# q before k in the attention by seven products: the order of the phases, the copies of q, and the queue of the bound's broadcast

## The chip, the cores and the metric

The kernel runs on one core of a Trainium2 chip. The metric is device time in microseconds of one execution. The times shown are those of three runs; the profile is one further execution, taken by the hardware profiler. The engines are named as in the profile: PE (TensorE) multiplies matrices, DVE (VectorE), ACT (ScalarE) and POOL (GpSimd) work on elements, SP (SyncE) only issues transfers. ACT, POOL and SP issue DMAs in the order of their own instruction streams: an instruction that waits holds up everything behind it on its engine.

## The reference

The input x has 2048 rows (tokens) of 1024. Four residual steps are applied to it: attention, token mixer, attention, token mixer, with the same weights both times.

```python
x = x + _A_ref(_layernorm(x, axis=-1), A_wqkv, A_wo)
x = x + _B_ref(_layernorm(x, axis=-1), B_w1, B_b1, B_w2, B_b2)
```

and the same two lines once more. `_A_ref` is attention with 32 heads of 32, in which a token sees itself and the seven tokens at distances 2, 4, ... 14 before it. Even and odd tokens therefore never meet, and the kernel treats them as two classes of 1024 tokens. `_B_ref` multiplies along the token axis: 2048 tokens to 3584 hidden units, gelu, and back.

## The kernel before

**Stages.** In the order of time: start-up with v of the first layer (0 to 64 us of the span), first attention (to 204), its output projection and layer norm (to 262), first `gemm1` (to 430), `gemm2f` (to about 620), the second layer's v and attention (to about 800), the last visits and the rest of the output projection (to 860), second `gemm1` (to 1032), `gemm2s` (to the end). Matrix products from the first `gemm1` on, and q, k and v of the second layer, are computed as Strassen-like schemes: seven products of half-size blocks in place of eight, with sums of blocks made beforehand on DVE and POOL, and partial results moved between PSUM banks by ACT.

**The second attention** is class `Attention` (L533). It works through NP = 8 periods. In period p two phases run, one for q and one for k, each for 256 columns (two groups of four heads) of one class of tokens. A phase is the seven products P1, P5, P6, P2, P7, P3 and P4, of four matmuls each (L652). ACT copies the bank of one product into the next bank before it is added to (`ab` and `pc`, L717), makes `Z` (L720), and writes out the corner blocks `c11` and `c21` (L724); DVE writes `y12` and `y22`, which add `Z` (L725). The four results of k go straight into their tile (`kT` or `kx`). The four results of q go into one tile `qs`, from which they are copied by DMA into the two buffers `qB` (L679): each result by four transfers, one a head, into that head's own place, since the rest of qB must stay zero. A DVE copy `hq` (L685) adds eight columns to the first buffer that lie over the border between its halves.

Between the products stand the visits of the pair before: in period p the steps S1 to S4 are the score products (L812) of the four visits of pair p - 1, `e` their exponentials on ACT (L820), `m` the multiplications by the band mask on DVE, four a visit (L836), V the products with v (L861 to L874), `l` and `x` the reciprocal of the sums on ACT, `n` the division on DVE (L887). V lags S by two visits. S1 and S2 read the first buffer qB (halves c11 and y12), S3 and S4 the second (c21 and y22). The four `t` steps of the first four periods make the block sums for the second class of tokens (L568).

**What sets the order.** The strings PE, ACT, DVE, SP and POOL (L535 to L539) give the order of the steps on each engine within a period, written out by hand; "-" means the step of the period before. `needs` (L589) tells which steps must be issued before a step, and `cycle` (L633) merges the strings accordingly. Each engine's instructions are chained in that order. Waits between engines are then set by the tile framework from what the instructions read and write. On POOL, `wk` and `wq` load the next weights and their sums (L571 to L576, two transfers of 512 KB each), which were stored to DRAM by `keep` (L527) ahead.

Before the change, k's phase comes first in a period: P1k, P4q of the period before, P5k, S1, V1, P6k, P2k, P7k, S2, V2, P3k, P1q, P4k, P5q, S3, V3, P6q, P2q, P3q, S4, V4, P7q. `last_visits` (L995) continues by hand after the last period: the remaining steps of period 7, then the output projection of the first eight tiles between the last visits. `out_proj` (L916) loads a residual tile `xr` three tiles ahead of its use.

**The bound's broadcast** belongs to the first `gemm1` (L1303). Its w1 blocks are scaled to fp16 by a power of two. For each block fb, DVE takes the maximum of both halves (`top`, L1322, two reductions); `share(fb)` (L1325) stores the 128 x 2 maxima to DRAM (`mxd`) and reads them back to all partitions (`bc`); one block later `power` reduces bc on DVE (L1233) and ACT scales the weights (L1332). Both transfers of `share` are issued by SP, whose queue also carries the loads of w1 (L1178), the stores of sums (L1348) and the loads for the second matrix's bound (L1286).

Of the kernel before, what the change touches and what calls it, by code (L numbers as in the profile page):

```python
# [9 lines left out]
ACT = mybir.ActivationFunctionType  # L10
# [7 lines left out]
P = 128  # L18
# [10 lines left out]
def kernel(  # L29
# [15 lines left out]
    nc = tc.nc  # L45
# [8 lines left out]
    NI = SC // P  # L54
    NG = D // P
# [442 lines left out]
    TURN = (2, 3, 0, 1)  # L498
# [33 lines left out]

    class Attention:  # L533
        NP = 4 * NG // 4
        PE = "P1k P4q- P5k S1 V1 P6k P2k P7k S2 V2 P3k P1q P4k P5q S3 V3 P6q P2q P3q S4 V4 P7q"  # L535
        ACT = "abk c21q- Zk e1a e1b l1 pck x1 e2a c11k l2 x2 abq e2b c21k e3a e3b l3 pcq x3 c11q Zq e4a l4 x4 e4b"
        DVE = ("n1 y22k m10 m11 y12k m12 n2 m13 m20 t1 m21 m22 m23 n3 m30 m31 y12q y22q hq m32 n4 m33 m40 t2 m41 m42 m43")
        SP = "dc21q- dc11q dy12q dy22q"
        POOL = "wk wq wx"  # L539

        def __init__(self):
# [26 lines left out]
            return tt(nc.vector, self.t_home(c, n)[:, ks], x[:, ks], y[:, ks], ALU.subtract)  # L568

        def load(self, phi):  # L570
            n = 2 * TURN[phi // 2 % (NG // 2)] + phi % 2  # L571
            ts = [wp.tile([P, KD, 256], FP16, name="Aq", tag="w"), wp.tile([P, 4, 4, P], FP16, name="Bq", tag="w")]
            self.w[phi] = [t[:] for t in ts]
            chain_("POOL", lambda: nc.gpsimd.dma_start(out=ts[0][:], in_=sdq[n][0]))
            chain_("POOL", lambda: nc.gpsimd.dma_start(out=ts[1][:].rearrange("p a k c -> p (a k c)"),
                                                       in_=sdq[n][1].rearrange("p k c -> p (k c)")))  # L576

        def take(self, phi, blocks):
            n = 2 * TURN[phi // 2] + phi % 2
            self.w[phi] = [blocks.R[n][:].bitcast(FP16), blocks.S[n][:]]  # L580

        def start(self, v, oT, wo):
# [5 lines left out]

        def needs(self, n, p):  # L589
            k, f = n[:-1], n[-1]  # L590
            o, d = ("q", p - 1) if f == "k" else ("k", p)
            if n[0] == "d":
                return [(n[1:], p)]
            if n[0] == "w":
                return {"x": [], "k": [("P4q", p - 1)], "q": [("P4k", p)]}[f]
            if n == "hq":
                return [("y12q", p)]
            if f in "kq":
                r = {"P1": [("c11" + o, d)], "ab": [("P1" + f, p), ("y12" + o, d)], "P5": [("Z" + o, d)],
                     "Z": [("P5" + f, p), ("y22" + o, d), ("y12" + o, d)], "P6": [("ab" + f, p)],  # L600
                     "pc": [("P6" + f, p), ("c21" + o, d)], "P2": [("ab" + f, p)], "P7": [("pc" + f, p)], "P3": [("pc" + f, p)],
                     "c11": [("P2" + f, p)], "y22": [("P7" + f, p), ("Z" + f, p)], "y12": [("P3" + f, p), ("Z" + f, p)],
                     "P4": [("y22" + f, p)], "c21": [("P4" + f, p)]}[k]
                if f == "q" and k in ("c11", "y12", "y22", "c21"):
                    r.append(("d" + n, p - 1))
                if k == "P1":
                    r.append(("wq", p - 2) if f == "k" else ("wk", p - 1))
                return r
            if n[0] == "t":
                return [("P5q", p)] if p == 3 else []  # L610
            c = n[1]
            o, d = {"1": ("4", p - 1), "2": ("1", p), "3": ("2", p), "4": ("3", p)}[c]
            if n[0] == "V":
                j = (int(c) - 3) % 4
                e = p - (c in "12")
                return [(f"m{j + 1}{r}", e) for r in range(4)] + [("l" + o, d), ("n" + o, d)]
            return {"S": [("e" + o + "a", d), ("e" + o + "b", d), ("dc11q", p - 1), ("dy12q", p - 1), ("hq", p - 1)]
                    + ([("dc21q", p - 1), ("dy22q", p - 1)] if c in "34" else []),
                    "e": [("S" + c, p)], "m": [("e" + c + "a", p), ("e" + c + "b", p), ("V" + c, p)],
                    "l": [("V" + c, p)], "x": [("l" + c, p)], "n": [("x" + c, p)]}[n[0]]  # L620
# [37 lines left out]
        def one(self, e, n, p):  # L658
            if e == "PE":
                in_order(self.do, n, p)  # L660
            elif n[0] == "d":
                self.do(n, p)
            else:
                chain_(e, self.do, n, p)
            self.done.add((n, p))
# [6 lines left out]
        def do(self, n, p):  # L672
# [24 lines left out]
            if f in "kq":  # L697
                ci_ = civ[:, 1:2]
                c = p // (NG // 2)
                bk = x.setdefault((f, p), {})  # L700
                if n[0] == "P":
                    A, B = self.w[2 * p + (f == "q")]
                    m = n[1]
                    if m in "15":
                        bk["pa" if m == "1" else "pd"] = bank("s")
                    lhs, rhs, out = {"1": (lambda: A[:, 0:4, 0:P], lambda: self.raw(c, 0, 0), "pa"),
                                     "2": (lambda: A[:, 4:8, 0:P], lambda: self.raw(c, 1, 0), "pa"),
                                     "5": (lambda: B[:, 0], lambda: self.t_home(c, 1), "pd"),
                                     "6": (lambda: B[:, 1], lambda: self.t_home(c, 2), "pb"),
                                     "7": (lambda: B[:, 2], lambda: self.t_home(c, 3), "pc"),  # L710
                                     "3": (lambda: B[:, 3], lambda: self.raw(c, 1, 1), "pb"),
                                     "4": (lambda: A[:, 4:8, P:2 * P], lambda: self.t_home(c, 4), "pc")}[m]
                    return self.product(bk[out][:], lhs(), rhs(), m in "15")
                if k in ("ab", "pc"):
                    o, i = ("pb", "pa") if k == "ab" else ("pc", "pb")
                    bk[o] = bank("m")
                    return nc.scalar.copy(out=bk[o][:], in_=bk[i][:])  # L717
                if k == "Z":
                    bk["z"] = x2("z", [P, 512], FP32)
                    return nc.scalar.activation(out=bk["z"][:], in_=bk["pd"][:], func=ACT.Identity, scale=ci_)  # L720
                a, b = int(k[1]) - 1, int(k[2]) - 1
                dst = self.place(f, p, a, b)
                if k[0] == "c":
                    return nc.scalar.activation(out=dst, in_=bk["pc" if a else "pa"][:], func=ACT.Identity, scale=ci_)  # L724
                return nc.vector.scalar_tensor_tensor(out=dst, in0=bk["pc" if a else "pb"][:], scalar=ci_, in1=bk["z"][:],  # L725
                                                      op0=ALU.mult, op1=ALU.add)
# [184 lines left out]
    def load_xr(res, e="SP"):  # L911
        t = gop.tile([P, D], BF16, name="xr", tag="go")
        xrs.append(t)
        chain_(e, lambda: (nc.sync if e == "SP" else nc.gpsimd).dma_start(out=t[:], in_=res(*todo.pop(0))))

    def out_proj(c, i, oT, wo, res, dst, h2, place=False):  # L916
        xr = xrs.pop(0)
        if todo:
            load_xr(res)
        if place:  # L920
            h2[c][i] = vhp.tile([P, D], BF16, name="h2", tag="vh")
        xn = h2[c][i] if place else x2("xn")
# [72 lines left out]
    def last_visits(at, v, oT, wo, res, dst, h2):  # L995
# [56 lines left out]
            chain_("DVE", divide, *divmod(z + n, 2), oT, accs[n], rds[n])  # L1052

        one = at.one
        one("DVE", "y22q", d)
        one("SP", "dy22q", d)
        one("DVE", "m32", d)
        one("DVE", "n4", d)
        o(0, 0)
        one("PE", "P4q", d)  # L1060
        one("ACT", "c21q", d)
        one("SP", "dc21q", d)
        a(0, 0)
        one("DVE", "m33", d)
        one("DVE", "hq", d)
        o(0, 1)
        a(0, 1)
        for r in range(4):
# [234 lines left out]
    def gemm1(h2, g, first):  # L1303
# [19 lines left out]
                                           apply_absolute_value=True)  # L1323

        def share(fb):  # L1325
            nc.sync.dma_start(out=mxd[fb], in_=bx[fb][:])
            bc_[fb] = pcp.tile([P, P * DIL], FP32, name="bc", tag="pc")
            nc.sync.dma_start(out=bc_[fb][:], in_=mxd[fb].rearrange("p c -> (p c)").partition_broadcast(P))

        def scale_w(fb, c):  # L1330
            w = w1s[fb][c]
# [660 lines left out]
    for li in range(2):  # L1992
# [77 lines left out]
        else:  # L2070
# [39 lines left out]
            at.late = {6: first_rows}  # L2110
            for k in range(2):
                at.take(2 + k, blocks[0])
                blocks[0].keep(6 + k, "POOL")
            oT = [None] * NG
            at.start(v, oT, wo)
            at.load(4)
            for p, e, m, j in ((p, f"t{j + 1}", m, j) for p, m in enumerate((3, 1, 2, 4)) for j in range(2)):
                at.extra[e, p] = lambda m=m, j=j: at.t_sum(1, m, j)
            for p in range(at.NP):
                if 1 <= p <= NG // 2:  # L2120
                    for k in range(2):
                        oT[2 * TURN[p - 1] + k] = gop.tile([P, S], BF16, name="oT", tag="go")
                if p == at.NP - 1:
                    at.DVE = at.DVE[:at.DVE.index(" y22q")]
                    at.SP = at.SP[:at.SP.index(" dy22q")]
                at.cycle(p)
            ahead_tiles = 8
            last_visits(at, v, oT, wo, res, xa[li], h2)
# [75 lines left out]
```

## Time and profile before

| | us |
|---|---|
| runs shown | 1204.96, 1208.30, 1208.88 |
| median | 1208.30 |
| profiled execution | 1207.63 |
| its span | 1205.9 |
| PE busy | 1174.4 |
| DVE busy | 804.9 |
| ACT busy | 741.6 |
| POOL busy | 157.7 |

The span is the time from the first to the last instruction in the profile; the 1.7 us around it belong to the execution. Of the stages, busy time of PE against length:

| stretch, us | length | PE busy |
|---|---|---|
| 262 to 430, first `gemm1` | 168.0 | 164.9 |
| 620 to 800, second attention | 180.0 | 166.0 |
| 800 to 860 | 60.0 | 57.4 |
| 860 to 1032, second `gemm1` | 172.0 | 171.3 |

A profile line of the timeline gives start, length, engine, line of the kernel, operation, output and inputs, and in brackets the idle time of that engine before it and what ended it. "PE s L812" is a matmul of line 812 that writes a bank named s. A releaser "DMA qB<-qs" is the landing of a transfer from qs to qB. "issue" means that the profile shows nothing that ended the wait.

### The profile page before, as it was taken

The numbers are of one execution on the slowest core, as the hardware profiler recorded it, in microseconds if no ns is written. First come the engines' busy times: TensorE is split into PE (matmuls) and PEld (weight loads), VectorE is DVE, ScalarE is ACT, GpSimd is POOL, SyncE is SP. The second block draws the span as 40 slices with busy tenths as digits, with TensorE's granted clock in tenths as the row PEclk, the third lists the DMA queues.
The fourth block names the chain that finished last, engine by engine and source line by source line (L and its number), as shares of the span: only waits on it lengthen the run. The fifth ranks groups of instructions, "written<-read, shape, count | busy, mean of one in ns | idle before, by whom it ended". The sixth has DMA issues, their size and how long they took to land.

```text
span 1205.9 us, 20563 instructions
## 1 busy us (share of the span) xinstructions
PE 1174.4 (97%) x7773; PEld 542.7 (45%) x7908; DVE 804.9 (67%) x1541; ACT 741.6 (61%) x1236; POOL 157.7 (13%) x159
## 2 busy tenths in 40 slices
PE   9999999999999999999999898999999999999998
PEld 4444444444444444444444344444444444444444
DVE  7558887887777546957678488787833432784663
ACT  4767876678878776665668477877543434432342
POOL 0000000281000031000040111201911212100000
PEclk9999999999999999999999899999999999999999
DMA  8922233696666778975465645535867755175521
GB/s 231 162 62 71 74 111 93 211 280 166 188 213 181 210 197 189 219 183 152 144 184 218 211 125 152 173 105 163 282 194 207 226 163 155 56 192 140 153 74 35
DMA packets 255859, 197.33 MB, mean 164 GB/s; under 512 B 50128, under 2 KB 226640, under 8 KB 252432
## 3 DMA queue, kind: packets, MB, share of 16 engines
q1 hardware_dynamic: 250912, 178.45, 53.6%
q0 software_dynamic: 4848, 17.57, 4.4%
q8 instruction: 62, 1.02, 0.4%
q14 instruction: 37, 0.30, 0.1%
HBM read 142.88 MB, written 38.82 MB: 151 GB/s over the span
## 4 chain that ended last, share of the span: by engine, by line
PE 88%; DMA 5%; ACT 2%; DVE 2%; issue 2%; SPq 1%; DVEq 0%; ACTq 0%
PE s L1356 11%; PE m L775 9%; PE m L927 8%; PE m L1356 7%; PE s L1565 7%; PE a L1356 6%; PE s L1715 5%; PE m L1565 4%; PE m L654 4%; PE a L1565 3%; PE s L654 3%; PE m L1715 3%; PE s L1195 2%; PE s L300 2%; PE s L450 2%; PE s L1808 2%
## 5 line engine op out<-in xcount | busy, mean ns | idle before, releaser
L836 DVE TENSOR_TENSOR Pm<-pc,band 32x640 bf16<-32x640 bf16 x256 | 125.2, 489 | 27.0 <-ACT pc L820 21.1
L1356 PEld LDWEIGHTS <-Sw 128*128 128x128 f16 x832 | 81.4, 98 | 100.9 <-issue 2.0
L775 PE MATMUL m<-hT,wqk 128*128 128x512 bf16 x481 | 111.8, 379 | 3.1 <-issue 2.2
L927 PE MATMUL m<-wo,oT 128*128 128x512 bf16 x497 | 111.3, 379 | 1.2 <-issue 0.5
L1356 PEld LDWEIGHTS <-w 128*128 128x128 f16 (+1 forms) x624 | 61.1, 98 | 73.6
L820 ACT ACTIVATE pc<-s,shift 128x320 bf16<-128x320 f32 x128 | 62.1, 527 | 28.6 <-PE s L812 28.1
L927 PEld LDWEIGHTS <-oT 128*128 128x128 bf16 x512 | 49.3, 98 | 60.8 <-issue 2.9
L775 PEld LDWEIGHTS <-wqk 128*128 128x128 bf16 x512 | 47.6, 98 | 59.0 <-issue 5.3
L1356 PE MATMUL s<-T,Sw 128*128 128x512 f16 x288 | 66.2, 379 | 1.9 <-ACT s L1365 1.9
L1209 POOL TENSOR_TENSOR Pm<-g 128x512 f16<-128x512 bf16 x24 | 28.6, 1208 | 285.8 <-ACT Pm L1290 165.8
L1209 DVE TENSOR_TENSOR py<-pz,m 128x512 f32<-128x512 f32 x14 | 9.6, 688 | 77.2 <-PE m L1356 63.1
L1209 POOL TENSOR_TENSOR T<-h 128x512 f16<-128x512 bf16 x16 | 18.4, 1152 | 288.3 <-ACT h L988 232.7
L887 DVE TENSOR_TENSOR oT<-a,rd 128x512 bf16<-128x512 f32 x64 | 44.2, 691 | 16.6 <-ACT rd L882 15.4
L1356 PE MATMUL m<-T,Sw 128*128 128x512 f16 x224 | 52.9, 379 | 0.4 <-ACT m L1365 0.4
L1356 PE MATMUL a<-h,w 128*128 128x512 bf16 x218 | 51.6, 379 | 0.4
L1332 ACT ACTIVATE w<-w,cs 128x2048 f16<-128x2048 bf16 x26 | 51.8, 1997 | 0.0
L1209 DVE TENSOR_TENSOR xs<-tq,xs 128x512 bf16<-128x512 f32 (+1 forms) x30 | 21.9, 732 | 44.3 <-ACT tq L1720 27.1
L1322 DVE TENSOR_REDUCE mx<-w 128x1 f32<-128x2048 bf16 x22 | 49.5, 2277 | 2.1 <-DMA w<-in_B_w_dram 2.0
L1565 PEld LDWEIGHTS <-u 128*128 128x128 f16 x336 | 32.9, 98 | 39.6
L1356 PE MATMUL s<-h,w 128*128 128x512 bf16 x186 | 44.1, 379 | 0.3
L1371 ACT ACTIVATE g<-pz,b_sb,ci 128x512 bf16<-128x512 f32 x26 | 21.1, 813 | 36.4 <-DVE pz L1209 36.4
L1209 DVE TENSOR_TENSOR py<-pz,s 128x512 f32<-128x512 f32 x12 | 8.3, 688 | 52.8 <-PE s L1356 43.7
(308 smaller groups left out, 2476.7 us busy)
## 6 DMA issues: line engine op xcount, KB each, us to landing
w<-in_B_w_dram SPq DMA_DIRECT2D x110, 512.0 KB, 6.0
sd<-Sw SPq DMA_DIRECT2D x13, 1024.0 KB, 8.1
Sw<-sd SPq DMA_DIRECT2D x13, 1024.0 KB, 4.9
xs<-xa SPq DMA_DIRECT2D x32, 256.0 KB, 3.3
Pm<-in_B_w_dram SPq DMA_DIRECT2D x26, 256.0 KB, 6.2
xa<-xn SPq DMA_DIRECT2D x24, 256.0 KB, 3.9
Aq<-sdq POOLq DMA_DIRECT2D x12, 512.0 KB, 3.8
Bq<-sdq POOLq DMA_DIRECT2D x12, 512.0 KB, 5.5
```

The source lines that it names most:

```text
L654: r = nc.tensor.matmul(out, lhsT=lhs[:, k, :], rhs=rhs[:, k, :], start=start and k == 0, stop=k == 3, skip_group_check=True)
L775: mm = nc.tensor.matmul(ps[:], lhsT=wts[part][:, kt, (g % 2) * P:(g % 2 + 1) * P], rhs=hT[:, kt, lo:lo + 512], start=(kt == 0), stop=(kt = ...
L820: return nc.scalar.activation(out=pc[:, 2 * n:2 * n + 2].rearrange("p t h k -> p (t h k)"), in_=ss[n][:, 0:2 * HG * GW], func=ACT.Exp, sca ...
L836: return nc.vector.tensor_tensor(out=Pm[rp, :, s0:s0 + HB, r * KG:r * KG + GW].rearrange("p h t k -> p t h k"), in0=pc[rp], in1=mk, op=ALU ...
L887: return nc.vector.tensor_tensor(out=oT[g][:, lo:lo + HB * P], in0=acc[0][:], in1=rd[:], op=ALU.mult)
L927: mm = nc.tensor.matmul(ps[:], lhsT=oT[g][:, cols(c, i)], rhs=wo[n][g // 4][:, g % 4, :], start=(g == 0), stop=(g == NG - 1))
L1209: return eng.tensor_tensor(out=out, in0=a, in1=b, op=op)
L1322: return nc.vector.tensor_reduce(out=bx[fb][:, c:c + 1], in_=w1s[fb][c][:], op=ALU.max, axis=AX.XY, apply_absolute_value=True)
L1332: return nc.scalar.activation(out=w[:].bitcast(FP16), in_=w[:], func=ACT.Identity, scale=cs[:, fb + 1:fb + 2])
L1356: r = nc.tensor.matmul(out, lhsT=lhs[:, k, :], rhs=rhs[k], start=start and k == 0, stop=stop and k == NI - 1, skip_group_check=True)
L1565: r = nc.tensor.matmul(out, lhsT=lhs[k], rhs=rhs[k][:, cols_], start=start and k == 0, stop=k == K - 1, skip_group_check=True)
L1715: r = nc.tensor.matmul(out, lhsT=lhs[k], rhs=rhs[k], start=start and k == 0, stop=k == K - 1, skip_group_check=True)
```

## The change

In `Attention`, q and k change places in every string and rule. q's phase runs first in a period, k's second; the weights are loaded and taken in that order (`load`, `take`). The copies of q are issued by SP in the order c21 and y22 of the period before, then c11 and y12 of this period, and `needs` places the first two behind S4 and the other two behind S2. `hq` moves ahead of m20 and behind S2. The block sums of the last kind (m = 4) take the places t2 and t3, the last at the end of DVE's string. `last_visits` issues the copies of c21 and y22 first and finishes k's y22 and c21 where q's were. One residual load in `out_proj` goes to POOL's queue. In `gemm1`, `share` issues its two transfers on POOL's queue for fb > 3, that is for ten of its eleven blocks.

```diff
-        PE = "P1k P4q- P5k S1 V1 P6k P2k P7k S2 V2 P3k P1q P4k P5q S3 V3 P6q P2q P3q S4 V4 P7q"
-        ACT = "abk c21q- Zk e1a e1b l1 pck x1 e2a c11k l2 x2 abq e2b c21k e3a e3b l3 pcq x3 c11q Zq e4a l4 x4 e4b"
-        DVE = ("n1 y22k m10 m11 y12k m12 n2 m13 m20 t1 m21 m22 m23 n3 m30 m31 y12q y22q hq m32 n4 m33 m40 t2 m41 m42 m43")
-        SP = "dc21q- dc11q dy12q dy22q"
+        PE = "P1q P4k- P5q S1 V1 P6q P2q P7q S2 V2 P3q P1k P4q P5k S3 V3 P6k P2k P3k S4 V4 P7k"
+        ACT = "abq c21k- Zq e1a e1b l1 pcq x1 e2a c11q l2 x2 abk e2b c21q e3a e3b l3 pck x3 c11k Zk e4a l4 x4 e4b"
+        DVE = "n1 y22q m10 m11 y12q m12 n2 m13 hq m20 t1 m21 m22 m23 n3 m30 m31 y12k y22k m32 n4 m33 m40 t2 m41 m42 m43 t3"
+        SP = "dc21q- dy22q- dc11q dy12q"
...
-            n = 2 * TURN[phi // 2 % (NG // 2)] + phi % 2
+            n = 2 * TURN[phi // 2 % (NG // 2)] + 1 - phi % 2
...
-            o, d = ("q", p - 1) if f == "k" else ("k", p)
+            o, d = ("k", p - 1) if f == "q" else ("q", p)
             if n[0] == "d":
-                return [(n[1:], p)]
+                return [(n[1:], p), ("S4" if n[2] == "2" else "S2", p)]
...
             if n == "hq":
-                return [("y12q", p)]
+                return [("y12q", p), ("S2", p)]
...
-            load_xr(res)
+            load_xr(res, "POOL" if place and i == NI - 1 else "SP")
...
-        one("DVE", "y22q", d)
+        one("SP", "dc21q", d)
         one("SP", "dy22q", d)
+        one("DVE", "y22k", d)
         one("DVE", "m32", d)
         one("DVE", "n4", d)
         o(0, 0)
-        one("PE", "P4q", d)
-        one("ACT", "c21q", d)
-        one("SP", "dc21q", d)
+        one("PE", "P4k", d)
+        one("ACT", "c21k", d)
         a(0, 0)
         one("DVE", "m33", d)
-        one("DVE", "hq", d)
...
         def share(fb):
-            nc.sync.dma_start(out=mxd[fb], in_=bx[fb][:])
             bc_[fb] = pcp.tile([P, P * DIL], FP32, name="bc", tag="pc")
-            nc.sync.dma_start(out=bc_[fb][:], in_=mxd[fb].rearrange("p c -> (p c)").partition_broadcast(P))
+            src = mxd[fb].rearrange("p c -> (p c)").partition_broadcast(P)
+            if fb > 3:
+                chain_(G, lambda: nc.gpsimd.dma_start(out=mxd[fb], in_=bx[fb][:]))
+                chain_(G, lambda: nc.gpsimd.dma_start(out=bc_[fb][:], in_=src))
+            else:
+                nc.sync.dma_start(out=mxd[fb], in_=bx[fb][:])
+                nc.sync.dma_start(out=bc_[fb][:], in_=src)
...
-            for p, e, m, j in ((p, f"t{j + 1}", m, j) for p, m in enumerate((3, 1, 2, 4)) for j in range(2)):
+            for p, e, m, j in ((p, f"t{j + 1 + (m == 4)}", m, j) for p, m in enumerate((3, 1, 2, 4)) for j in range(2)):
...
                 if p == at.NP - 1:
-                    at.DVE = at.DVE[:at.DVE.index(" y22q")]
-                    at.SP = at.SP[:at.SP.index(" dy22q")]
+                    at.DVE = at.DVE[:at.DVE.index(" y22k")]
```

## The prediction

> **What bounds the kernel now.** I read the busy table first, then the releasers of PE's idle time, then the PE timeline around those places, then busy time by stretch and the chain of work. In the busy table PE stands at 97%:
>
> ```profile
> PE 1174.4 (97%) x7773; PEld 542.7 (45%) x7908; DVE 804.9 (67%) x1541; ACT 741.6 (61%) x1236; POOL 157.7 (13%) x159
> ```
>
> So of a span of 1205.9 us only 31.5 us are idle PE, and no reordering can give more than that and what a lowered clock takes. The PE timeline (start, length, instruction; in brackets the idle time before it and what ended it) shows where most of it lies, in the second layer's attention:
>
> ```profile
> 678.00 0.73 PE L812 MATMUL s<-qB,kT 128*32 128x160 bf16 x16 [4.86 <-DMA qB<-qs]
> ...
> 714.11 0.46 PE L812 MATMUL s<-qB,kT 128*32 128x160 bf16 x16 [1.70 <-DMA qB<-qs]
> ...
> 732.09 0.46 PE L812 MATMUL s<-qB,kx 128*32 128x160 bf16 x16 [1.75 <-DMA qB<-qs]
> ...
> 753.52 0.46 PE L812 MATMUL s<-qB,kT 128*32 128x160 bf16 x16 [1.43 <-issue]
> ```
>
> Every line is a score step (S1, and at 753.52 S2) that waits for q to be copied by DMA from qs into qB. Three more follow, S2 at 770.37 (0.38), S1 at 783.76 (0.73) and S2 at 787.83 (0.43). The timeline names other releasers for some, but in each the last transfer that S2 or S1 reads lands just ahead of it (753.43 before 753.52, 783.63 before 783.76, 787.74 before 787.83), so I take all seven for waits on q: 11.28 us. The same stretch by busy time (us, then each engine, the granted clock, DMA share, GB/s):
>
> ```profile
> 673.10:678.00 4.90, 0.04 (x2) 0.03 (x2) 0.00 (x0) 0.69 (x1) 0.00 (x0) 0.89 1.04 372
> 678.00:683.80 5.80, 5.80 (x28) 2.04 (x28) 0.00 (x0) 1.51 (x3) 0.00 (x0) 0.50 0.64 206
> ...
> 732.10:748.20 16.10, 15.78 (x220) 7.70 (x224) 12.55 (x27) 13.29 (x25) 2.08 (x4) 1.00 0.44 132
> ```
>
> After the 4.86 us wait the clock is granted at 0.50 for 5.8 us: another 2.9 us. The third line is a whole pair without a wait: 16.1 us is what PE's own work costs, where pairs with a wait take 17.7 to 18.1.
>
> The other PE gaps that the change can reach are in the first layer's gemm1: 0.45 us before 399.67 and 1.95 before 413.87. The chain of work leads the second back to the bound's broadcast:
>
> ```profile
> 379.64 10.18 DMA mxd<-mx
> 389.84 5.54 DMA bc<-mxd
> 395.38 8.46 DMA mxd<-mx
> 403.86 5.33 DMA bc<-mxd
> ...
> 409.21 0.43 DVE m L1233
> ...
> 413.33 0.50 ACT s L1365
> ```
>
> The store of the maxima lies 10 us in SP's queue, the broadcast 5 more, DVE's reduction of bc waits, `pz` and ACT's copies queue behind it, and PE waits for the copy. The DVE waits are 0.55, 1.83 and 1.31 us, growing late in the stage.
>
> **Part 1, q first.** Nothing is added: the products, copies and transfers are the same in number. q's c11 and y12, which S1 and S2 of the next pair read, are made in the first half of a pair, and c21 and y22, which S3 and S4 read, are sent once S4 (S2 for the others) has left the buffer. In time of a 16.1 us pair counted from S1, c11 is ready at about 3.2 and y12 at 5.6; eight issues at 0.63 us each end near 8, and the row of pairs 2 to 5 gives the landing:
>
> ```profile
> DMA to landing us min/median/max: 1.8/2.2/4.8
> ```
>
> They land by 13, three us before the next S1; S2 has three more. c21 goes out from about 8.5, y22 after S4 (11.6), issued by 14.4; even at 4.8 us it lands at 18.6, that is 2.5 into the next pair, and S3 reads at 8. k is written by ACT and DVE straight into its tile, without a transfer, so being late in the pair costs it nothing: c11 of k is ready at 11, S1 is at 16. So the six waits after the first (1.70, 1.75, 1.43, 0.38, 0.73, 0.43) go: 6.42 us.
>
> **What is late next.** The DVE list now has y22q ahead of m10 to m13, and y22q overwrites qs, so it waits until the last transfer of y22 has landed. Queued behind it are the masks that V3 reads (four at 0.48), y12q, and P4q, which adds into the bank that y22q reads. In steady pairs y22q starts at 3.74 (735.83 against S1 at 732.09), and the landing above is at 14.4 - 0.6 + 2.2 = 16.0 (median) to 18.6 (slowest), that is -0.1 to 2.5: in time. DVE's work in a pair with class sums (second and third): 16 masks with their gaps 8.2, four divisions 2.8, four y 3.0, the four small copies 0.7, two sums 1.4, together 16.0 against 16.1. It fits with nothing to spare; bounds 0 (the row at 732 has 12.6 in 16.1, without sums) and 1.7 a pair (the old wait comes back as a wait for masks). I take 0.5 in all, nearer the row that fits.
>
> **The first pair.** Products run every 0.86 us. From 659.0 the first c11 of q is copied at 662.4 (where k's is now), y12 at 664.3; SP can issue 16 transfers from 663.2 to 672.7. The row of the start is slower, since 6 MB of weights are in flight:
>
> ```profile
> DMA to landing us min/median/max: 3.5/5.8/6.7
> ```
>
> c11's last lands at 665.1 + 5.8 = 670.9; S1 can start at 673.1, where PE falls idle now. So the 4.86 us go, and with them the 2.9 of half clock: 7.8. But y22's last transfer, issued at 672.7, lands at 678.5, and y22q of the next pair ends at 679.25, while P4q would run at 673.1 + 0.35 + 2.6 + 0.4 + 1.7 = 678.2. PE waits 1.1 there; the masks then end at 682.05 and V3, due at 681.4, waits 0.65. A new loss of 1.7; bounds 0 (landing in 3.5) and 3.5 (6.7, and SP held up by its eight transfers in flight, as its ninth issue waits for the first landing now).
>
> **Part 2, bound by GpSimd.** Ten stores and ten broadcasts go from SP's queue to POOL's. POOL has finished its sums at 275.4 and waits for nothing until 414, so nothing there is delayed. SP loses 65.3 us of waiting for mxd (eleven times, one remains), so loads and stores behind it go earlier. From the second maximum's end to the need of bc there are 14.9 us (367.0 to 381.9) to 16.2. No row has a small transfer on POOL's queue beside a full SP queue; from below, 2.2 us landing each (small transfers, little traffic), 0.54 issue, 5.5 in all; from above, the slowest of SP's own, 10.6 + 6.0, 17.7 with issues. Nearest is the reverse case, small SP transfers beside a full POOL queue, 5.8 us: 12.7, inside 14.9. Both gaps go: 2.4 us. DVE's next wait is for PE.
>
> The issue of a weight load on POOL's queue took 537 to 540 ns in all eight cases of 702 to 764, while DVE was busy over 75% of the time. Against this part speaks the Trainium skill, SBUF — State Buffer, "SBUF: two separate sides": GpSimd cannot write descriptors while DVE holds the shared port in a two-port mode, and such a transfer should be issued by SP. The trace shows no sign of it; by that rule two issues could each be held for a DVE instruction, which is the third rival below.
>
> **Costed at nothing.** hq (0.67) moves into DVE's first half; m20 to m23 end at 10.05 in the free pair, V4 reads at 11.8, so 1.1 is left. The sums m=4 one place later: P4q reads them at 6.2 of the fourth pair, the last ends near 3.9. One xr load (256 KB) on POOL waits for its buffer ahead of the sums of gemm1: the first two may slip from 813 to 826, but the third is due at 827.9 and from 848 POOL runs through to 874.7 anyway. At the end of attention S has no wait now; the 0.85 and 1.13 us before V at 820 and 830 come from masks behind the output adds and stay.
>
> **Sum**, against the profiled execution (1207.63 = span 1205.9 and 1.7 around it; the median of the runs is 1208.3, 0.7 above): 4.86 + 2.9 + 6.42 - 1.7 - 0.5 + 2.4 = 14.4, so **1193 us**.
>
> **Rivals.**
> - First pair stays late. PE's waits of 1.75 us left the clock at 1.00, that of 4.86 lowered it after 3.8. If y22 lands 2.7 us later than I say, P4q idles 3.8 and the half clock returns: 3.8 + 0.65 + 2.9 in place of 1.7, time 1199. The Trainium skill, TensorE: Matmul & The Clock Gate, Part 1, puts the limit at an idle window of about 3.4 us, free-running; the 3.8 here agrees, and by it 0.4 us less lateness would do. For: 372 GB/s there now; against: the transfers start six us earlier. Chance 0.12.
> - DVE becomes the bound: 1.7 lost in each of two pairs in place of 0.5, time 1196. For: 16.0 of 16.1; against: the waits on ACT's rd that leave DVE idle now (10 us in 696 to 784) are slack. Chance 0.13.
> - The broadcast stays late. Were the issues of store and broadcast each held by one 2.28 us reduction (L1322, the longest on DVE there), 12.7 + 4.6 = 17.3 is past the 14.9 and the 2.4 us are not won: 1196. For: DVE is busy over 70% of that stage; against: the uniform 537 to 540 ns. Chance 0.08.
> - y22q is late in every pair. It decides from a landing over 6 us after issue (4.8 the slowest so far); two us late in six pairs is 12 lost, time 1205, no change. Chance 0.05.
> - Slower: the GpSimd queue is the slow one. If store and broadcast take the 17.7 us above, bc is 1.5 to 2.8 late in each of ten blocks, where it is late in three now. From 14.9 on it decides; ten times 2.2 is 22, with the 2.4 not won, 1193 + 2.4 + 22 = 1217. For: nobody's row excludes it; against: POOL's ring is empty. Chance 0.05.
> - The change does not do what it says (S1 still waits for a transfer): the order of instructions shows S1's transfers eight issues earlier, so no more than 0.02, at 1205 to 1207 (gemm1's 2.4 or nothing).
>
> **Chances.** Forecast 0.55. With neither of the two new losses (1.7 and 0.5) the time is 1191, with the first rival 1199; the runs shown lie 2 us to either side of their middle, so the range is 1189 to 1201. It takes in the first three rivals (0.33); the others (0.12) are left out. A measurement of this kernel tells about 0.3% (3.6 us) from no change: faster 0.88 (0.55 + 0.33), same 0.06, slower 0.06.
>
> **What would show it.** Right: no idle PE before L812 between 673 and 800; PEclk 1.00 there; pairs of 16.1; one gap before P4q (L654) near 678 with DVE's qs waiting for DMA; no DVE wait for bc. Wrong: PE waiting at L861 for Pm in the second and third pair (DVE bound), a clock of 0.5 near 680, or DVE's L1233 line waiting for bc in early blocks.

## The result

The changed kernel takes **1201.28 us** (median of six runs, 1199.97 to 1202.24) against 1208.26 beside it, a ratio of 0.9948 (0.9932 to 0.9963). On another chip the two stood at 1199.46 and 1203.37, a ratio of 0.9965 (0.9952 to 0.9977). So the change is a gain, of 4 to 7 us, and half or less of the 15 us that were forecast; the time lies just above the range of 1189 to 1201.

The profiled execution took 1201.25 us with a span of 1199.5. Its busy table shows PE with the same work in a shorter span:

```profile
PE 1175.6 (98%) x7773; PEld 543.8 (45%) x7908; DVE 806.6 (67%) x1541; ACT 740.8 (62%) x1236; POOL 169.1 (14%) x180
```

I set the two traces beside each other at four points that both have. The lead is how much earlier the changed kernel gets there:

| point | before | after | lead | won on the way | forecast |
|---|---|---|---|---|---|
| attention's first product | 659.00 | 656.24 | 2.76 | 2.8 | 2.4 |
| S1 of the second pair | 695.95 | 693.18 | 2.77 | 0.0 | 6.1 |
| S (L812) ahead of the last rows | 806.45 | 797.06 | 9.39 | 6.6 | 5.9 |
| end of the span | 1205.9 | 1199.5 | 6.4 | -3.0 | 0 |

Two stretches did as forecast, and two did not. The PE timeline of the changed kernel shows the first of these, the first pair:

```profile
671.62 0.46 PE L812 MATMUL s<-qB,kT 128*32 128x160 bf16 x16 [1.25 <-DMA qB<-qs]
...
680.48 1.87 PE L654 MATMUL m<-Tq,Rq 128*128 128x512 f16 x4 [3.47 <-DVE qs L725]
...
693.18 0.46 PE L812 MATMUL s<-qB,kx 128*32 128x160 bf16 x16
```

S1 waits 1.25 us where it waited 4.86. But P4q then waits 3.47 us for DVE's `y22q`, which itself waits for a transfer of the first pair's q out of qs. The view of the tile qs has DVE's wait:

```profile
L725 DVE SCALAR_TENSOR_TENSOR qs<-m,civ,z x1: 752/752/752, 679.7 to 679.7; 128x512 bf16<-128x512 f32 x1
...
  DMA qB<-qs: 10.6, 1
```

The four matmuls of P4q take 1.87 us where others of the group take 1.03: the clock is halved again. The table by stretches shows it (us, the engines, granted clock, DMA share, GB/s):

```profile
676.07:679.48 3.41, 0.95 (x5) 0.31 (x4) 0.00 (x0) 0.13 (x1) 0.00 (x0) 1.00 0.98 318
679.48:682.89 3.41, 2.41 (x6) 0.86 (x6) 3.10 (x6) 0.71 (x2) 0.00 (x0) 0.50 0.08 24
682.89:686.30 3.41, 3.41 (x45) 1.55 (x44) 3.23 (x10) 2.42 (x5) 0.00 (x0) 0.50 0.19 52
...
819.43:822.84 3.41, 0.71 (x25) 0.46 (x25) 3.34 (x10) 0.00 (x0) 0.00 (x0) 1.00 0.00 0
822.84:826.25 3.41, 3.19 (x8) 1.22 (x8) 0.86 (x4) 3.32 (x5) 0.88 (x1) 0.50 0.23 82
```

The last two lines are the second loss, at the end of attention. There PE stands still for 3.57 us and the clock is halved a second time. The timelines of PE, DVE and POOL around it:

```profile
822.13 0.42 PE L861 MATMUL a<-Pm,v 128*32 128x136 bf16 x16 [3.57 <-DVE Pm L836]
```

```profile
815.32 4.46 DVE L836 TENSOR_TENSOR Pm<-pc,band 32x640 bf16<-32x640 bf16 x2 [0.27 <-ACT pc L820]
```

```profile
814.99 0.55 POOL L914 DMA_DIRECT2D xr<-xb  x1 [40.35 <-PE a L874]
815.55 3.37 POOL L1208 TENSOR_TENSOR T<-h 128x512 f16<-128x512 bf16 x3
```

Two masks take 4.46 us; the first of them alone took 3.96, where a mask takes 0.48. It starts while POOL issues the xr load, and ends 0.36 us after the third of three sums that POOL runs behind that load without a pause.

### The profile page after: what moved, and what is told of

Its sections match the earlier page's. It is cut to its first block, busy times and chain, and to the rows that moved or that the text cites. A ratio compares the mean times of both kernels' runs of the same rounds, so it can differ in the third digit from the quotient of the medians.

```text
span 1199.5 us, 20561 instructions
## 1 busy us (share of the span) xinstructions
PE 1175.6 (98%) x7773; PEld 543.8 (45%) x7908; DVE 806.6 (67%) x1541; ACT 740.8 (62%) x1236; POOL 169.1 (14%) x180
## 4 chain that ended last, share of the span: by engine, by line
PE 92%; DMA 2%; DVE 2%; ACT 1%; issue 1%; SPq 0%; DVEq 0%; ACTq 0%
PE s L1360 12%; PE m L775 9%; PE m L927 9%; PE m L1360 8%; PE s L1569 7%; PE a L1360 6%; PE s L1719 5%; PE m L1569 4%; PE s L300 3%; PE m L654 3%; PE a L1569 3%; PE m L1719 3%; PE s L1194 2%; DMA qB<-qs 2%; PE s L654 2%; PE s L450 2%
## 5 line engine op out<-in xcount | busy, mean ns | idle before, releaser
L879 ACT ACTIVATE rd<-a 128x512 f32<-128x512 f32 x64 | 38.5, 602 | 6.0 <-PE a L874 6.0
```

## The experiments

The theory: (1) in the first pair q's transfers share the DMA engines with eight weight loads (4 MB) and land late, and `y22q` must wait for them before it may overwrite qs; (2) the xr load, moved to POOL, holds back three token sums, which then run in one bunch and keep DVE's mask waiting. Rivals: SP's issuing sets the first pair's landings; the sums meet the masks whatever issues xr. Ratios are to the kernel before on the same chip, which took 1203.4 to 1204.2 us there. Three chips were used: one for xr by SP, y22 through kx, loads held and bound by SP again; one for the changed kernel again, sums later, both edits together and before with loads held; one for the last two of the kernel before. Times of two chips are compared below where it says so.

| kernel | us | ratio | interval |
|---|---|---|---|
| changed kernel again | 1199.46 | 0.9965 | 0.9952 to 0.9977 |
| xr by SP | 1196.90 | 0.9944 | 0.9930 to 0.9957 |
| sums later on POOL | 1195.74 | 0.9930 | 0.9915 to 0.9944 |
| y22 through kx | 1195.37 | 0.9932 | 0.9919 to 0.9944 |
| loads held | 1191.48 | 0.9895 | 0.9882 to 0.9909 |
| loads held, sums later | 1190.16 | 0.9885 | 0.9871 to 0.9898 |
| bound by SP again | 1201.92 | 0.9981 | 0.9971 to 0.9992 |
| before, loads held | 1202.07 | 0.9986 | 0.9978 to 0.9995 |
| before, bound by POOL | 1204.22 | 1.0000 | 0.9990 to 1.0009 |
| before again | 1203.50 | 0.9991 | 0.9982 to 1.0000 |

An edit can move both losses, so the total does not say what one of them is worth. The next table cuts one profile of each kernel at the points of the table above (us): when attention's first product starts, from there to S1 of the second pair, from there to the S ahead of the last rows, and from there to the end of the span. The first loss is read in the third column, the second in the last.

| kernel | first product | first pair | later pairs | to the end |
|---|---|---|---|---|
| before | 659.0 | 37.0 | 110.5 | 399.5 |
| changed kernel | 656.2 | 37.0 | 103.9 | 402.5 |
| changed kernel again | 656.3 | 36.3 | 103.7 | 402.4 |
| xr by SP | 656.1 | 35.0 | 103.7 | 399.2 |
| sums later on POOL | 656.4 | 37.0 | 104.3 | 397.5 |
| y22 through kx | 656.3 | 31.5 | 103.7 | 403.5 |
| loads held | 656.8 | 30.7 | 104.1 | 398.8 |
| loads held, sums later | 656.1 | 30.7 | 104.2 | 397.5 |
| bound by SP again | 656.9 | 37.0 | 103.9 | 402.7 |
| before, loads held | 656.9 | 33.0 | 110.9 | 399.5 |
| before, bound by POOL | 656.2 | 35.9 | 112.6 | 399.1 |
| before again | 656.5 | 37.3 | 109.6 | 399.5 |

**The weight loads held.**

```diff
                 phi = 2 * p + (3 if f == "k" else 4)
+                if phi == 5:
+                    lo = (HG - 1) * DH
+                    chain_("POOL", lambda: nc.gpsimd.tensor_copy(out=warm[lo:lo + DH, 0:1], in_=qB[1][lo:lo + DH, HG - 1, SC - 1:SC]))
```

> The changed kernel with a copy of 32 x 1 elements on POOL ahead of the reloads of q's and k's weights for the third pair and the fourth (six loads, 3 MB); it reads the last element that the first pair's last y22 transfer writes, so that these loads start only when that transfer has landed. Theory A: the first pair's transfers are late (5.5 to 9.1 us from issue to landing) because they share the DMA engines with these loads (312 to 372 GB/s between 665 and 680). Then c11's last lands some 3 us after its issue and S1 has no wait (1.25 now), y22's last lands before 675, P4q's wait of 3.47 goes to 0.5 or less, the clock stays at 1.00 and the time is 1201.3 - (1.25 + 3.0 + 2.9) = 1194. Rival B: SP's own sixteen issues, through eight transfers in flight, set it: landings and waits stay within 1 us of those now and the time is 1201. Rival C: the held weights come late for the third pair: a new wait before its products near 690 to 705, time 1197 or more.

Measured: 1191.48, some 8 us under the changed kernel (of two chips). PE's timeline has S1 with 0.50 us, P4q with no wait and S3 with 0.38:

```profile
671.42 0.46 PE L815 MATMUL s<-qB,kT 128*32 128x160 bf16 x16 [0.50 <-DMA qB<-qs]
...
676.65 1.03 PE L654 MATMUL m<-Tq,Rq 128*128 128x512 f16 x4
...
679.17 0.35 PE L815 MATMUL s<-qB,kT 128*32 128x160 bf16 x8 [0.38 <-ACT pc L823]
```

The next two fences are the same stretch, without and with the hold (the last three columns are clock, DMA share, GB/s):

```profile
670.00:675.00 5.00, 3.75 (x46) 1.64 (x44) 0.00 (x0) 2.44 (x5) 0.00 (x0) 1.00 1.04 362
```

```profile
670.00:675.00 5.00, 4.48 (x49) 1.92 (x48) 0.00 (x0) 3.00 (x6) 0.00 (x0) 1.00 0.29 68
```

SP issues y22's four transfers at the same time in both, 671.95 to 673.85 and 671.82 to 673.64. What differs is the landing. In the tile view of qB with the loads held, those four:

```profile
DMA to landing us min/median/max: 1.8/1.8/1.9
```

In the changed kernel `y22q` is released by the landing at 679.6, 5.7 us after the last issue began, and the tile view of Aq shows what stood in the way:

```profile
DMA to landing us min/median/max: 7.2/11.1/14.7
```

So it is the traffic that makes y22 land late, and not SP's issuing: theory A, and the first rival falls. c11's four are issued beside the two loads that are not held and the last stores of the weights, and still take up to 8.3 us; that is the 0.50 that S1 waits. The held loads came in time: no product of the later pairs waits. Not all of the 8 us belongs to the first pair. That stretch is 6.3 us shorter than in the changed kernel's first profile, and the end is 3.7 us shorter, since the mask met the sums otherwise there: PE waits 1.62 us for it in place of 3.57, and the clock stays at 1.00. This second part was not expected.

**y22 of the first pair through kx.**

```diff
+            if (p, a, n) == (0, 1, 1):
+                return kts[0][3][:, 512:]
             return self.qs[:, 2 * a + n]
...
-                                                           in_=self.qs[hp, 2 * a + b, lo:]))
+                                                           in_=self.place("q", p, a, b)[hp, lo:]))
```

> The changed kernel with y22 of the first pair's q written to the second half of the second kx tile, which nothing uses before the second pair's k, and copied to qB from there; all else as it is. So the second pair's y22q on DVE has no transfer to wait for. Theory A: P4q's wait of 3.47 us is only that buffer wait. Then P4q follows its predecessor, S3 waits instead for the landing of y22 at 679.5, where it is due at about 679: 0 to 0.8 us; the half clock after 679 (6.8 us at 0.50, 2.9 us of time) does not come: 1201.3 - (3.47 - 0.7 + 2.9) = 1195.6. Rival B: the lateness of the transfers only moves to S3 and V3: a wait of over 2.5 us in one piece there, the half clock stays, 1200 to 1201.

Measured: 1195.37. The transfers land no earlier, but nothing waits for them before S3 does:

```profile
679.89 0.23 PE L814 MATMUL s<-qB,kT 128*32 128x160 bf16 x1 [0.47 <-DMA qB<-kx]
```

So P4q's 3.47 us were a wait for the buffer, and the half clock after 679 hung on that wait; it did not come, and the first pair is 5.5 us shorter. The second half clock, after the mask, was there still, and longer than in the changed kernel (6.8 us from 815.45).

**xr by SP again.**

```diff
-            load_xr(res, "POOL" if place and i == NI - 1 else "SP")
+            load_xr(res)
```

> The changed kernel with one part undone: the xr load near the end of attention is issued by SP again, not by POOL. Theory A: on POOL that load waits for its buffer until 814.99, three token sums of 1.15 us queue behind it and then run back to back, and the mask of 0.48 us that starts in the same 0.3 us is held for 3.96 us until they end; PE waits 3.57 and the clock is 0.50 for 3.4 us. Then here the longest mask there is 1.36 again, PE waits about 0.85 and 1.13 as before the change, no half clock near 820, and the time is 1201.3 - (3.57 + 1.7 - 1.98) = 1198.0. Rival B: the sums meet anyway because attention as a whole runs earlier, whoever issues xr: the mask of about 4 us stays and the time is 1201. Rival C: xr on SP comes late for the output adds and PE waits there instead: 1200 to 1203, with waits on m in place of Pm.

Measured: 1196.90, with the two masks at 1.36 us each and PE's waits 0.85 and 1.13, as before the change. The wait of P4q stood there as in the changed kernel (3.48). The end is 3.3 us shorter than in the changed kernel's first profile, as expected. By the times the gain is 2.6 us (medians of two chips, with intervals that just overlap), so rivals B and C fall by the trace more than by the time.

**The sums later.**

```diff
-            for i in range(NI):
+            for i in range(NI) if first else (3, 0, 1, 2, 4, 5, 6, 7):
                 chain_(G, tt, nc.gpsimd, T[:, 0, i, :], B12[i], B11[i], ALU.subtract)
```

> The changed kernel with the order of eight token sums on POOL in the second layer altered: the sum of the fourth token block first, then those of the first three, so that behind the xr load (which stays on POOL) nothing runs there until about 825. Theory A: it is the bunch of sums that holds the mask on DVE. Then no mask takes over 0.6 us between 795 and 825, PE waits for Pm neither at 810 nor at 820, no half clock there: 1201.3 - 3.57 - 1.7 = 1196 at 1208.3 for the kernel before, so 5 us under the changed kernel; the bunch now runs near 826 and may hold one output add for up to 3 us, off PE's path. Rival B: it is the issue of the xr load by POOL (0.55 us, in which the mask begins) that holds the mask: the mask of about 4 us stays, same time as the changed kernel.

Measured: 1195.74, 3.7 us under the changed kernel on the same chip (5 expected). DVE's and POOL's timelines:

```profile
815.93 0.98 DVE L836 TENSOR_TENSOR Pm<-pc,band 32x640 bf16<-32x640 bf16 x2 [0.27 <-ACT pc L820]
```

```profile
815.61 0.55 POOL L914 DMA_DIRECT2D xr<-xb  x1 [40.01 <-PE a L874]
822.67 5.60 POOL L1208 TENSOR_TENSOR T<-h 128x512 f16<-128x512 bf16 x5 [6.52 <-ACT h L961]
```

Again two masks begin within 0.4 us of the issue of xr by POOL, and now they take 0.98 together. So the sums held the mask, and not the issue of the load. PE waits over 0.25 us for no mask from 790 to 830, and the 0.85 and 1.13 us that the kernel before had are gone as well. The end is 4.9 us shorter than in the changed kernel's profile on that chip, as expected; 0.6 us is lost again in the first pair, where the half clock lasted 6.8 us and not 3.4, and 0.7 in the later pairs.

**Both, the fastest version.** The two edits above, the hold and the sums.

> The changed kernel with both: the reloads held until the first pair's y22 has landed, and the fourth token block's sum first on POOL. Theory A: the two losses are independent, so the 1.62 us that PE still waited near 813 with the loads held goes too: 1.6 us under that run, 9.5 to 11 us under the changed kernel, PE idle for under 1.5 us in waits over 0.25 us between 660 and 830. Rival B: something else comes in its place (an output add held by the bunch of sums, m banks late): no better than with the loads held alone.

Measured: 1190.16, 1.15% under the kernel before and 9.3 us under the changed kernel on the same chip, 1.3 under the loads held alone (of two chips, with intervals that overlap). Waits of PE of 0.25 us or more between 660 and 830: 0.25, 0.42 and 0.31. Theory A; the two stretches are each as short as in the better of the two single edits.

**The changed kernel again.**

> The changed kernel itself, unaltered, beside the kernel before and the variants on one chip. In the first set of variants the kernel before took 1204.2 us where it took 1208.3 beside the changed kernel, so times of two sets can be compared by their ratios alone. Theory A: the ratio is the one measured, 0.995 (0.993 to 0.996), so the variants with a ratio of 0.9944 (xr by SP), 0.9932 (y22 through kx) and 0.9895 (loads held) are worth 0.5, 2 and 6.5 us. Rival B: the kernel before takes 1204 or 1208 by how its half clock falls, and here the changed kernel stands at 1201 against 1204, a ratio of 0.997: then the three are worth 3, 5.5 and 9.5 us.

Measured: 0.9965, the number of rival B, though not for the reason it gives: the kernel before has the same length of half clock in both of its profiles (below). The changed kernel's profile shows the same two waits, 4.18 and 3.57, and two half clocks of 3.4 us each.

**The kernel before with the loads held.** The edit is that of the first experiment.

> The kernel before with the reloads of the third and fourth pairs' weights held until the last transfer of y22 of the first pair has landed, as in the run that held them in the changed kernel; the order of q and k stays as before. Theory A: with the loads out of the way q's transfers land 2 to 3 us after their issue, but y12's are issued last and late (672.5 to 674.3), so S1 still waits until about 677: 3.4 to 4 us in place of 4.86, and the later waits (6.42) stay. Gain 1 to 1.5 us, or up to 2.9 more where the clock is then not halved: ratio 0.996 to 0.999. Rival B: the loads are the whole cause of the first wait, and the hold alone gives as much as in the changed kernel: ratio 0.993 or less.

Measured: 0.9986, so the hold alone is worth 1.3 us, where in the changed kernel it is worth 8. The number is as expected, the place of the wait is not:

```profile
672.11 0.46 PE L815 MATMUL s<-qB,kT 128*32 128x160 bf16 x16 [0.83 <-ACT z L723]
...
681.38 0.46 PE L815 MATMUL s<-qB,kT 128*32 128x160 bf16 x16 [2.15 <-DMA qB<-qs]
```

S1 waits 0.83 and S3 2.15, and the clock is not halved. So the hold does shorten the first pair in the old order too, by 4.3 us against the kernel before's second profile; 1.3 of it are lost again in the later pairs, where the waits of S sum to 6.5 us against 5.2, for a reason that stays open. S3's wait seems to come with the edit itself, which was not tested: in the old order c21 is issued behind y22, and its last transfer (677.45) went out as the held loads started (677.47) and took 3.7 us to land, where the eleven ahead of it took 1.8 to 1.9. With the loads out of the way the change is worth about 10 us, by the two profiles with the loads held: 2.3 in the first pair, 6.8 in the later ones, 0.7 at the end.

**The bound's broadcast**, by SP again in the changed kernel and by POOL alone in the kernel before:

```diff
-            if fb > 3:
+            if fb > 99:
                 chain_(G, lambda: nc.gpsimd.dma_start(out=mxd[fb], in_=bx[fb][:]))
```

> The changed kernel with store and broadcast of the bound on SP's queue again in every block. Theory A: the move to GpSimd's queue is worth what the gaps of the first layer's gemm1 were, 0.45 + 1.95 us less the 0.25 left, and a little more as attention began 2.76 us earlier: 1201.3 + 2.1 to 2.8 = 1203.4 to 1204.1, with PE waiting for m and s copies near 399 and 412. Rival B: the gaps went with something else and the time is 1201.

> The kernel before with one part of the change alone: store and broadcast of the bound from the fifth block on go by GpSimd's queue, attention as before. Theory A: it is worth the gaps in gemm1 that the kernel before has on this chip less 0.25: 0.3 to 0.6 us by the profiles of the variants with SP's broadcast (0.53 and 0.81 idle at 411), so a ratio of 0.9985 to 1.000; the broadcast lands 11 to 16 us after the store's issue as in the changed kernel. Rival B: 2.4 us as forecast from the first profile, ratio 0.998 or less.

> The kernel before itself, unaltered, for a second profile: on the chips of the variants it takes 1203.3 to 1204.2 us, where it took 1208.3 beside the changed kernel. Theory A: the difference lies in waits that differ from one execution to the next, gemm1's broadcast (2.4 us in the first profile; 0.25 to 0.8 in every profile of the variants, also where the bound is sent by SP) and the length of q's waits with the half clock behind. Then this profile shows under 1 us of idle PE between 395 and 415, and the wait ahead of the first S1 or the half clock behind it is shorter than 4.86 and 6.8 us. Rival B: the same waits stand there and the work itself is shorter (PE's busy time under 1174 by 3 us or more).

Measured: 1201.92, 1204.22 and 1203.50. Taken out of the changed kernel the move costs 2.5 us by the medians (of two chips, with intervals that overlap), of which its profile shows 0.28 in gemm1 (0.53 for 0.25, and not the 2.1 or more that were expected), and about 1.1 as a longer half clock behind P4q's wait than in the changed kernel's repeated profile (6.83 us for 3.41). Added to the kernel before it gives nothing that can be measured. PE's timeline there, first without and then with the move:

```profile
411.89 1.89 PE L1356 MATMUL s<-T,Sw 128*128 128x512 f16 x8 [0.96 <-ACT s L1365]
```

```profile
411.26 1.89 PE L1361 MATMUL s<-T,Sw 128*128 128x512 f16 x8 [0.26 <-ACT s L1370]
```

The gap goes, as forecast, but it was 0.96 us in this execution and not the 2.40 of the first profile. Apart from that first profile, attention starts only 0.3 us (kernel before) and 0.7 us (changed kernel) sooner with the move than without. This also answers part of why the kernel before took 1208 on one chip and 1203 on others: it reached the first S1's wait 2.3 us sooner, 1.4 of it from this gap. Against expectation, q's first wait was not shorter (5.14, with 6.8 us of half clock). Where the rest comes from stays open; on the first chip itself, two of the six runs of the kernel before took 1205.0 and four 1208.2 to 1208.9.

## Why the prediction was wrong

By its own steps:

- **gemm1, +2.4.** Right for the profile it was made from: the gap left is 0.25. From the store's issue to the landing of bc it took 10.8 to 16.5 us, 12.7 forecast; one of the eleven reductions of bc on DVE waited, 0.50 us, and PE did not wait for it. But the size came from one execution; the repeated profile of before has 0.96 to win.
- **The six later waits, +6.42.** Right. No S waits for a transfer after 671.62, and the pairs run at their own cost:

```profile
709.56:725.77 16.21, 15.89 (x226) 7.80 (x230) 14.47 (x30) 13.82 (x26) 2.15 (x5) 1.00 0.55 163
725.77:741.95 16.18, 15.86 (x221) 7.70 (x224) 15.12 (x31) 13.79 (x26) 2.14 (x5) 1.00 0.52 156
```

- **DVE nearly full, -0.5.** Right in kind: 15.1 busy of 16.2, one wait for a mask over 0.25 us (0.29 at 783.17).
- **First pair, +4.86 + 2.9 - 1.7.** This step failed: nothing came of the 6.1 us. The mechanism was named ("lands at 678.5", "PE waits 1.1 there"); its two times were off, each by about 1.2 us. y22's landing was at 679.6, since the traffic stood in the way and SP's sixteen issues took 14 us, not 9.5: three took 1.1 to 1.65 us, and the twelfth (671.39) waited 1.2 us until the fourth transfer had landed, 9.1 us after its issue.

  P4q was due at 677.0 and not 678.2, since PE came to attention 2.76 us sooner; SP's first issue came as much sooner (660.5 for 663.2), its last ended later (674.4 for 672.7). 1.1 became 3.5, as much as the upper bound set on the whole new loss.

  S1, which was to wait for nothing, waited 1.25: c11's last transfer landed at 671.4 for 670.9, and PE was there at 670.4 and not at 673.1. I let the clock fall only from 3.8 us of idleness; 3.47 were enough, and the 2.9 us came back. So 1.25 + 3.47 + 2.9 = 7.6 us came in the place of the 4.86 + 2.9 that went.

  The 2.4 us won in gemm1 were added to the gains of this stage as if both could be had; at a wait that ends with a transfer that comes no sooner, an earlier arrival only lengthens the wait. The sign named for this, "a clock of 0.5 near 680", came: it was the rival "First pair stays late", at 1199, with a chance of 0.12.
- **The xr load, costed at nothing.** This step failed too. I followed the load and the buffer, wrote that the first sums "may slip from 813 to 826", and asked whether they would still be in time for `gemm1`, which they were. I did not ask what three sums in one bunch do to DVE. The chain of work of before had the row, two masks of 1.36 us, each starting 0.14 us after one such sum of 1.15 had begun on POOL:

```profile
818.18 1.36 DVE Pm L836
...
828.05 1.36 DVE Pm L836
```

Their cost is in the waits of 0.85 and 1.13 that I called masks "behind the output adds". Price: 3.57 + 1.7 - 1.98 = 3.3, by the table -3.0.
- **Slower, and y22q late in every pair.** Neither came; from the second pair on no product waits for `y22q`.

The sum with what was measured: 2.8 + 0.0 + 6.6 - 3.0 = 6.4. Right in direction; either of the two failed steps alone would have left the time inside the range.

## What to carry to other kernels

Where a transfer is moved earlier, look at what else is in flight at that time: an issue that comes earlier need not land earlier while large loads are in flight (y22's last transfer took 5.7 us here, and 1.8 without the loads), and gains ahead of such a wait do not add to it. A DMA put on an engine that also computes holds back that engine's work while the DMA waits for its buffer, and the work then runs in a bunch (here three sums); ask what the bunch meets on the other engines. Repeat the profile before pricing a gap of a microsecond.

## What the runs showed of the hardware

**The half clock comes in windows of its own.** All stretches at 0.50 in these profiles, but the last of each span, last 3.41 or 6.83 us, and within a profile they lie whole multiples of 3.41 apart. What goes with them is how busy PE was in the window before: with 0 to 1.25 us busy the next window was at 0.50. The border lies near 1.5: below are the two windows in which P4q's wait lay with xr by SP, which kept the clock, and one with a wait of only 1.88 us in the kernel with the bound by POOL, which lost it. It is no sharp border in these figures, some of whose matmul records are missing: a window of the first profile of before with 1.46 (from 410.72) kept the clock too.

```profile
674.93:678.34 3.41, 1.68 (x8) 0.73 (x9) 0.00 (x0) 1.02 (x2) 0.00 (x0) 1.00 1.04 360
678.34:681.75 3.41, 1.51 (x8) 0.68 (x7) 2.27 (x4) 0.00 (x0) 0.00 (x0) 1.00 0.32 93
```

```profile
726.23:729.64 3.41, 1.53 (x44) 0.80 (x43) 3.31 (x7) 1.71 (x4) 0.39 (x1) 1.00 0.86 295
729.64:733.05 3.41, 3.41 (x10) 1.21 (x9) 0.72 (x2) 1.80 (x4) 0.00 (x0) 0.50 0.26 66
```

At 0.50 it took more to return: windows with 1.48 to 2.41 us busy stayed there, those with 2.83 and more did not. So a wait of 3.5 us cost nothing more (P4q's with xr by SP, 3.48), 1.7 us (the mask's in the changed kernel, 3.57) or 2.9 us (P4q's there, 3.47), by where it fell among the windows. The Trainium skill, TensorE: Matmul & The Clock Gate, Part 1, gives a free-running window of 3413 ns, and the traces agree; its condition, an idle window, is too strict, since one with 1.25 us of work in it was enough.

**A run of POOL instructions can hold a DVE instruction through all of them.** A mask that began during the issue ahead of three sums was held for 3.96 us in four profiles (changed kernel twice, y22 through kx, bound by SP). It is not always so. With the loads held, two masks met the same bunch:

```profile
809.77 1.84 DVE L839 TENSOR_TENSOR Pm<-pc,band 32x640 bf16<-32x640 bf16 x2 [0.28 <-ACT pc L823]
```

```profile
809.44 0.55 POOL L917 DMA_DIRECT2D xr<-xb  x1 [40.19 <-PE a L877]
810.05 3.69 POOL L1211 TENSOR_TENSOR T<-h 128x512 f16<-128x512 bf16 x3
```

The first began at the same point of the issue, 0.33 us in, and took its 0.48; the second, 0.2 us after the first sum had begun, took 1.35 and let the second sum wait (1.40 in place of 1.15). What decides between the two is not shown. The Trainium skill, SBUF — State Buffer, "SBUF: two separate sides", describes a port pair that DVE or GpSimd locks for a whole instruction, whichever starts first. That one waits for the other agrees; that a mask whose record starts 0.23 us ahead of the first sum's can lose against three sums in a row is more than the section says. The half of it that I had weighed, GpSimd's issues held by DVE, showed in no row: stores and broadcasts were issued in 0.54 to 0.56 us, but for one of 0.71.
